# A second sequence's attention placed later in the first feed-forward layer: preparation of its first pair of heads in six steps of its own, its jobs from a third of the layer on

## The chip, the cores and the metric

The kernel runs on one core of a Trainium2 chip. The metric is the device time of one execution in microseconds (us): lower is better. Before the change the median of 3 runs is 1101.23 us.

## What is computed

Attention over 4 sequences of 576 tokens with 8 heads of 64 columns, where a score counts only if it lies within `tau` of its row's greatest, and then two feed-forward layers over the 2304 tokens (512 columns, 2048 hidden):

```python
scores = scale * np.matmul(q, k.transpose(0, 1, 3, 2))
scores = np.where(scores >= max(scores) - tau, scores, -1e9)
attn = softmax(scores)
x = np.matmul(attn, v)                        # to (2304, 512)
h = x @ w_in;  x = (h * clip(h + 3, 0, 6) / 6) @ w_out       # layer 1
h = x @ w2_in; r = maximum(h, 0); out = (r * r) @ w2_out     # layer 2
```

The four weight matrices arrive as 64-bit floats and are turned on the chip into pairs of 16-bit floats, a high and a low part.

## The kernel before, in words

**Attention.** A unit is a pair of heads of one sequence; there are 16, u0 to u3 for the first sequence, u4 to u7 for the second, and so on. A unit has nine jobs (128 queries each, one of them the two heads' tails). `run` (L422) writes the jobs out in steps: step i writes `scores` (L272) and `soft1` (L290) of job i, `soft2` (L305) of job i-1, and `av` (L328) of job i-LAG with LAG = 5. In a job TensorE makes the scores `s` in a PSUM tile of the pool `ps_s`, VectorE takes the row's extreme `nm` (L293), ScalarE the exponential (L303), VectorE the threshold and row sum (L310, which frees `s`), ScalarE and GpSimd the high and low part (L316 to L318), SyncE's queue a transposing DMA into `pt` (L320), and TensorE the product with v (L342).

A unit has to be prepared first (`prep_steps`, L182): TensorE transposes `kraw` and `qraw` (L176) in four parts into tiles called `tps`, ScalarE and VectorE copy them out. In the first sequence units are plain, a copy by ScalarE (L192, L199, L201). From the second sequence on they are kept as a rounded value and a remainder, so each part costs a ScalarE and a VectorE instruction for each head (L212, L213, L222, L223); two DMAs double k (L226), and `prep_v` (L231) scales v. One preparing step is taken for each job of the unit ahead, so u4 is prepared during u3's jobs, and it is handed over from the first `run` to the second (L419, L420). The `tps` tiles of u4, and of u4 alone, come from `ps_s` (L171), three tiles that it shares with `s`; all others come from `ps_a`. A unit's k, q and v are loaded by SyncE's queue (L153 to L168) during jobs 2, 4 and 6 of the unit two ahead: u4's during u2's, u5's during u3's.

**The feed-forward layers.** A block is one layer for one sequence, in the order 1_0, 2_0, 1_1, 2_1 and so on (L752). A block has 16 hidden tiles `hp` (L657) in four quads, and after each quad four output tiles `y` (L694); each tile is 24 matmuls and comes from `ps_s` too. The first hidden tile of the next quad stands ahead of a quad's outputs. Each tile gives two yields, and layer 1 ends with BUBBLE = 8 more yields while its result is scaled and split (L709, L378, L379). That is 72 yields for block 1_0.

**The weights.** In the first sequence's blocks, `tick` (L612) and `want_w` convert a weight tile some tiles ahead of its use: a 1 MB load (L502, L505), VectorE's reduction (L521), a scale by way of TensorE (L118), ScalarE, VectorE, ScalarE and GpSimd instructions (L583 to L595), and a store of 512 KB for the later sequences (L597). Blocks 1_0 and 2_0 convert 16 tiles each; the first two are written out among the last jobs of the first sequence (L769), and after step 34 (L772) four loads and the scaling of the first three quarters of x follow.

**The order of the work.** At L778 41 steps have been written: the 36 jobs of the first sequence and LAG steps more. Then the blocks are written tile by tile, and after each yield `attn_to` (L799) writes as many further steps as an even spread asks for. For block 1_0 the spread is FIRST_ATT = 15 steps over its 72 yields (L789), so that the second sequence's first job is written with the first tile. Block 2_0 gets 26 steps over 56 yields. The framework places each engine's instructions with a schedule of its own, so the order on an engine is near to the written one and not always equal to it.

Of the kernel before, what the change touches and what calls it, by code (L numbers as in the profile page):

```python
# [26 lines left out]
FIRST_ATT = 15  # L27
EARLY = {2: 0, 3: 1, 4: 2, 5: 3, 6: 5, 7: 7}
# [10 lines left out]
def attention_moe_moe_kernel(  # L39
# [130 lines left out]
    def transpose_part(t, part, wide=False):  # L170
        if wide:  # L171
            a = ps_s.tile([P, 2, 512], F32, tag="s", name="tps")[:, 0]
        else:
            a = ps_a.tile([P, 512], F32, tag="acc", name="tps")
        for i, j in enumerate((0, 1) if part == 0 else (2, 3, 4)):
            nc.tensor.transpose(a[:, i * P:i * P + P], t[:, j].rearrange("p h d -> p (h d)"), ident)  # L176
        return a
# [4 lines left out]
    def prep_steps(u):  # L182

        u.plain = u.b == 0
        if u.plain:
# [3 lines left out]
            for part in (0, 1):  # L189
                a = transpose_part(u.k, part, u.i == NPAIR)  # L190
                c0, n = cols(part)
                nc.scalar.activation(out=u.kf[:, c0:c0 + n], in_=a[:, 0:n], func=AF.Copy)  # L192
                yield
            for part in (0, 1):
                a = transpose_part(u.q, part, u.i == NPAIR)
# [11 lines left out]
        for part in (0, 1):  # L207
            a = transpose_part(u.k, part, u.i == NPAIR)
            c0, n = cols(part)
            for h in range(2):  # L210
                kh = u.ks[h][own[h], 0, c0:c0 + n]
                nc.scalar.activation(out=kh, in_=a[own[h], 0:n], func=AF.Copy)  # L212
                nc.vector.tensor_tensor(out=u.ks[h][own[h], 1, c0:c0 + n], in0=a[own[h], 0:n], in1=kh.bitcast(F32), op=ALU.subtract)  # L213
            yield
        for part in (0, 1):
            a = transpose_part(u.q, part, u.i == NPAIR)
# [174 lines left out]
    def attention():  # L391
# [27 lines left out]
        pr = yield from run(us, all_jobs[0:n], None)  # L419
        yield from run(us, all_jobs[n:], pr)  # L420

    def run(us, all_jobs, pr):  # L422
        n = len(all_jobs)
        for i in range(n + LAG):
            if i < n:
                j = all_jobs[i]
                if j.first:
# [3 lines left out]
                    pr = prep_steps(us[j.u.i + 1]) if j.u.i + 1 < len(us) else None  # L431
# [21 lines left out]
            if i < n and all_jobs[i].u.i + 2 < len(us):  # L453
# [8 lines left out]
        return pr  # L462
# [294 lines left out]
    need = {f"1_{b}": (b + 1) * 9 * NPAIR + (LAG if b else 0) for b in range(B)}  # L757
# [21 lines left out]
    for i, (tag, layer, b) in enumerate(blocks):  # L779
# [8 lines left out]
        if i == 0:  # L788
            ng, todo = 4 * NF + BUBBLE, FIRST_ATT  # L789
# [7 lines left out]
        for g, _ in enumerate(moe(tag, layer, b, xs)):  # L797
            if nxt is not None:
                attn_to(min(nxt + LAG, start + math.ceil(todo * (g + 1) / ng)))  # L799
# [30 lines left out]
```

## Time and profile before

| | us |
|---|---|
| median of 3 runs | 1101.23 (1100.09 to 1102.97) |
| the profiled execution | 1104.33 |
| its span (first to last instruction) | 1102.5 |
| first sequence's attention, to the first tile `hp` | 0 to 102 |
| block 1_0 | 102 to 273 |
| block 2_0 | 273 to 422 |

Busy times in the profile are sums over one execution of one engine: PE is TensorE's matmuls, PEld its weight loads, DVE VectorE, ACT ScalarE, POOL GpSimd, and SPq SyncE's queue, which issues nearly all DMAs. PEclk is TensorE's granted clock as a share of its full 2.4 GHz (0.50 is 1.2 GHz). The DMA share is that of the 16 DMA engines, and can pass 1 where transfers overlap. An engine's idle time counts only where something later waits for it.

### The profile page before, as it was taken

How to read it: one execution, taken by the hardware profiler on the slowest of the kernel's cores; microseconds unless marked ns; L12 is line 12 of the kernel's file. 1: busy time of each engine (PE TensorE's matmuls, PEld its weight loads, DVE VectorE, ACT ScalarE, POOL GpSimd, SP SyncE). 2: the span in 40 equal slices, each digit the busy share in tenths (PEclk: the TensorE clock that was granted, in tenths of full speed). 3: DMA queues.
4: the chain of work that ended last, by engine and by line, in shares of the span. 5: the costliest groups of instructions: out<-in, count | busy, mean ns of one | idle time of the engine just before them, and what ended most of it. 6: DMA issues, size and time to landing. Idle time of an engine off the chain costs nothing.

```text
span 1102.5 us, 23355 instructions
## 1 busy us (share of the span) xinstructions
PE 1008.4 (91%) x9248; PEld 817.0 (74%) x9248; DVE 644.1 (58%) x1344; ACT 654.2 (59%) x1128; POOL 500.7 (45%) x613
## 2 busy tenths in 40 slices
PE   6867587986998999999999999999899999998998
PEld 4646465775777878878788888888688887776776
DVE  5788599677778785455855564555835231224122
ACT  6878599676887875655576465755554344213222
POOL 6867178654555763434354443444444212212111
PEclk9998699997999999999999999999999999999999
DMA  6998999787686886665566656556455342222211
GB/s 143 161 215 188 311 277 325 242 257 177 174 207 184 174 204 178 124 146 135 132 134 138 147 139 153 131 120 142 86 129 118 103 130 82 96 77 77 78 39 44
DMA packets 264126, 168.66 MB, mean 153 GB/s; under 512 B 221264, under 2 KB 233552, under 8 KB 264016
## 3 DMA queue, kind: packets, MB, share of 16 engines
q1 hardware_dynamic: 262688, 166.83, 60.7%
q8 instruction: 73, 1.20, 0.5%
q10 hardware_dynamic: 1328, 0.33, 0.1%
q14 instruction: 37, 0.30, 0.1%
HBM read 99.62 MB, written 21.50 MB: 110 GB/s over the span
## 4 chain that ended last, share of the span: by engine, by line
PE 64%; DVE 14%; ACT 8%; DMA 8%; issue 2%; POOL 2%; SPq 1%; ACTq 0%; POOLq 0%; DVEq 0%
PE y L694 28%; PE hp L657 27%; PE s L287 3%; PE o L342 3%; DMA wd<-in_moe_w_in_dram 3%; DVE wc L592 2%; DMA wd<-in_moe_w_out_dram 2%; DVE nm L293 2%; DVE g L521 2%; ACT wc L583 2%; DMA vraw<-in_v_dram 1%; DVE e L310 1%; DVE ya L700 1%; DMA pt<-p 1%; PE tps L176 1%
## 5 line engine op out<-in xcount | busy, mean ns | idle before, releaser
L657 PE MATMUL hp<-x,wpi 128*128 128x288 f16 x3072 | 400.7, 289 | 18.1 <-DVE e L310 5.0
L657 PEld LDWEIGHTS <-wpi 128*128 128x128 f16 x3072 | 298.1, 99 | 97.3 <-issue 9.5
L694 PEld LDWEIGHTS <-wpo 128*128 128x128 f16 x3072 | 296.7, 98 | 85.7 <-issue 6.3
L694 PE MATMUL y<-gh,wpo 128*128 128x288 f16 x2048 | 335.7, 287 | 9.8 <-DVE ya L700 3.5
L668 POOL TENSOR_TENSOR gl<-g,gh 128x576 f16<-128x576 f32 x128 | 168.9, 1322 | 285.0 <-ACT gh L667 284.4
L694 PE MATMUL y<-gl,wpo 128*128 128x288 f16 x1024 | 208.1, 287 | 0.1
L293 DVE TENSOR_REDUCE nm<-s 128x1 f32<-128x576 f32 x144 | 107.9, 751 | 56.3 <-PE s L287 50.6
L700 DVE SCALAR_TENSOR_TENSOR ya<-y,yq,ya 128x576 f32<-128x576 f32 (+1 forms) x97 | 77.8, 808 | 95.3 <-PE y L694 94.8
L318 POOL TENSOR_TENSOR p<-e,p 128x512 f16<-128x512 f32 x108 | 127.1, 1177 | 0.0
L667 ACT ACTIVATE gh<-g 128x576 f16<-128x576 f32 x128 | 86.5, 679 | 57.2 <-DVE g L662 29.2
L310 DVE SCALAR_TENSOR_TENSOR e<-s,thr,e 128x576 f32<-128x576 f32 x108 | 88.0, 815 | 41.7 <-ACT e L303 40.7
L342 PE MATMUL o<-v,pt 128*128 128x64 f16 (+1 forms) x2016 | 92.4, 202 | 13.2 <-DMA pt<-wpo 4.1
L342 PEld LDWEIGHTS <-pt 128*128 128x128 f16 x2016 | 82.4, 101 | 25.0 <-issue 9.4
L316 ACT ACTIVATE p<-e 128x576 f16<-128x576 f32 x108 | 73.6, 682 | 45.5 <-DVE e L310 36.8
L287 PE MATMUL s<-k_st,q_st 128*128 128x288 f32 x480 | 94.1, 319 | 5.7 <-DVE e L310 1.5
L665 DVE TENSOR_TENSOR g<-g,hp 128x576 f32<-128x576 f32 x64 | 48.0, 751 | 66.2 <-ACT g L664 66.0
L661 ACT ACTIVATE g<-hp,r_h,aq 128x576 f32<-128x576 f32 x64 | 52.9, 828 | 55.0 <-PE hp L657 54.5
L662 DVE SCALAR_TENSOR_TENSOR g<-g,r_w,hp 128x576 f32<-128x576 f32 x64 | 51.8, 810 | 54.9 <-ACT g L661 54.8
L664 ACT ACTIVATE g<-hp,r_w 128x576 f32<-128x576 f32 x64 | 47.1, 735 | 59.5 <-PE hp L657 58.4
L317 POOL TENSOR_TENSOR p<-e,p 128x64 f16<-128x64 f32 x108 | 35.0, 324 | 103.0 <-issue 66.2
L303 ACT ACTIVATE e<-s,nm 128x576 f32<-128x576 f32 x108 | 78.3, 725 | 0.4
L287 PEld LDWEIGHTS s<-k_st,q_st 128*128 128x128 f32 x480 | 69.5, 190 | 10.1 <-issue 3.4
(124 smaller groups left out, 1085.0 us busy)
## 6 DMA issues: line engine op xcount, KB each, us to landing
wpi<-scr SPq DMA_DIRECT2D x48, 512.0 KB, 3.8
wpo<-scr SPq DMA_DIRECT2D x48, 512.0 KB, 3.9
wd<-in_moe_w_in_dram SPq DMA_DIRECT2D x16, 1024.0 KB, 6.6
wd<-in_moe_w_out_dram SPq DMA_DIRECT2D x16, 1024.0 KB, 6.5
scr<-wpi SPq DMA_DIRECT2D x16, 512.0 KB, 5.2
scr<-wpo SPq DMA_DIRECT2D x16, 512.0 KB, 4.9
kraw<-in_k_dram SPq DMA_DIRECT2D x16, 256.0 KB, 4.0
vraw<-in_v_dram SPq DMA_DIRECT2D x16, 256.0 KB, 3.2
```

The lines of the kernel that those rows point to most:

```text
L287: nc.tensor.matmul(s[:, half, 0:HALF], lhsT=u.qs[sl][:, cs], rhs=u.ks[sl][:, kk, c], start=i == 0, stop=i == len(ops) - 1)
L293: nc.vector.tensor_reduce(out=j.nm, in_=j.s, axis=AX.XY, op=ALU.min)
L303: nc.scalar.activation(out=j.e, in_=j.s, func=AF.Exp, bias=j.nm, scale=-1.0)
L310: nc.vector.scalar_tensor_tensor(out=j.e, in0=j.s, scalar=j.thr, in1=j.e, op0=ALU.is_le, op1=ALU.mult, accum_out=u.sm[:, col:col + 1])
L316: nc.scalar.activation(out=p16[:, 0:S], in_=e, func=AF.Copy)
L318: nc.gpsimd.tensor_tensor(out=p16[:, S + TAIL:], in0=e[:, 0:NT * P], in1=p16[:, 0:NT * P], op=ALU.subtract)
L342: nc.tensor.matmul(o[:, n * w:n * w + w], lhsT=j.pt[:, c, :], rhs=vv[:, hs, vc, :], start=i == 0, stop=i == len(ops) - 1)
L657: nc.tensor.matmul(hp[:, a, 0:HALF], lhsT=wsl(tag, "i", f, w, c), rhs=x[c][:, a * HALF:(a + 1) * HALF], start=i == 0, stop=i == 3 * NC - 1)
L667: nc.scalar.activation(out=gh, in_=gf, func=AF.Copy)
L668: nc.gpsimd.tensor_tensor(out=gl, in0=gf, in1=gh, op=ALU.subtract)
L694: nc.tensor.matmul(a[:, k_, 0:HALF], lhsT=wsl(tag, "o", f, w, e), rhs=g[f][:, k_ * HALF:(k_ + 1) * HALF], start=i == 0, stop=i == len(ops) ...
L700: nc.vector.scalar_tensor_tensor(out=y, in0=av_, scalar=yq, in1=y, op0=ALU.mult, op1=ALU.add)
```

## The change

The first `run` ends with the first sequence: it neither loads u4 and u5 nor prepares u4. After it come six steps (PRE = 6) that hold no job: the first issues u4's loads of k and q, the next five take the five preparing steps of u4, and four of these also issue, one each, u4's v and u5's k, q and v. Then the second `run` follows as before. In block 1_0 nothing is written of these steps until yield 24 (FIRST_AT, after hidden tile 8, a third of the block); the 6 + 15 steps are spread over the remaining 48 yields. So the first job is written at yield 37. At the end of block 1_0 the same jobs have been written as before, and from block 2_0 on the spread is the same (26 steps over 56 yields). The transposed tiles of u4 come from `ps_a` like all others.

```diff
+FIRST_AT = 24
+PRE = 6
...
-    def transpose_part(t, part, wide=False):
-        if wide:
-            a = ps_s.tile([P, 2, 512], F32, tag="s", name="tps")[:, 0]
-        else:
-            a = ps_a.tile([P, 512], F32, tag="acc", name="tps")
+    def transpose_part(t, part):
+        a = ps_a.tile([P, 512], F32, tag="acc", name="tps")
...
-        pr = yield from run(us, all_jobs[0:n], None)
-        yield from run(us, all_jobs[n:], pr)
-
-    def run(us, all_jobs, pr):
+        yield from run(us, all_jobs[0:n], NPAIR)
+        load_qk(us[NPAIR], "k")
+        load_qk(us[NPAIR], "q")
+        yield (0, 0)
+        nxt = [lambda: load_v(us[NPAIR])] + [lambda x=x: load_qk(us[NPAIR + 1], x) for x in "kq"] + [lambda: load_v(us[NPAIR + 1])]
+        pr = prep_steps(us[NPAIR])
+        for _ in range(PRE - 1):
+            next(pr, None)
+            if nxt:
+                nxt.pop(0)()
+            yield (0, 0)
+        assert next(pr, 1) == 1 and not nxt
+        yield from run(us, all_jobs[n:], len(us))
+
+    def run(us, all_jobs, stop):
         n = len(all_jobs)
+        pr = None
...
-                    pr = prep_steps(us[j.u.i + 1]) if j.u.i + 1 < len(us) else None
+                    pr = prep_steps(us[j.u.i + 1]) if j.u.i + 1 < stop else None
...
-            if i < n and all_jobs[i].u.i + 2 < len(us):
+            if i < n and all_jobs[i].u.i + 2 < stop:
...
-    need = {f"1_{b}": (b + 1) * 9 * NPAIR + (LAG if b else 0) for b in range(B)}
+    need = {f"1_{b}": (b + 1) * 9 * NPAIR + (LAG + PRE if b else 0) for b in range(B)}
...
         if i == 0:
-            ng, todo = 4 * NF + BUBBLE, FIRST_ATT
+            ng, todo = 4 * NF + BUBBLE - FIRST_AT, PRE + FIRST_ATT
...
             if nxt is not None:
-                attn_to(min(nxt + LAG, start + math.ceil(todo * (g + 1) / ng)))
+                x = g + 1 if i else g + 1 - FIRST_AT
+                attn_to(min(nxt + LAG, start + math.ceil(todo * x / ng)))
```

## Rows read from the trace of the kernel before

**Rows 1.** The page's head and busy times of the whole span.

```profile
span 1102.5 us, 23355 instructions
PE 1008.4 (91%) x9248; PEld 817.0 (74%) x9248; DVE 644.1 (58%) x1344; ACT 654.2 (59%) x1128; POOL 500.7 (45%) x613
```

**Rows 2.** Busy time by stretch: PE, PEld, DVE, ACT, POOL; then PEclk, DMA share, GB/s.

```profile
30.00:63.00 33.00, 25.78 (x259) 19.05 (x256) 24.87 (x58) 27.02 (x60) 25.23 (x51) 1.00 0.96 161
63.00:102.00 39.00, 26.93 (x255) 19.45 (x254) 34.03 (x82) 33.36 (x70) 28.20 (x46) 0.87 0.95 208
102.00:129.00 27.00, 16.32 (x163) 13.22 (x162) 17.54 (x38) 14.44 (x26) 10.83 (x17) 0.77 1.03 281
129.00:176.00 47.00, 38.80 (x275) 29.21 (x274) 40.56 (x86) 42.11 (x60) 29.62 (x24) 0.92 0.99 300
176.00:259.00 83.00, 75.06 (x661) 59.83 (x662) 66.69 (x126) 63.16 (x92) 54.18 (x48) 0.96 0.82 246
259.00:273.00 14.00, 5.65 (x55) 4.90 (x53) 11.01 (x31) 9.74 (x13) 6.94 (x7) 0.65 0.82 233
273.00:422.00 149.00, 137.09 (x1369) 113.56 (x1368) 116.45 (x259) 116.96 (x204) 88.92 (x99) 0.99 0.76 182
```

**Rows 3.** Tiles `k_st`, then `q_st`, 63 to 102 us: PE, PEld, DVE, ACT, POOL.

```profile
63.00:102.00 39.00, 0.00 (x0) 0.00 (x0) 1.80 (x4) 1.61 (x4) 0.00 (x0) 0.87 0.95 208
63.00:102.00 39.00, 0.00 (x0) 0.00 (x0) 2.50 (x6) 2.48 (x6) 0.00 (x0) 0.87 0.95 208
```

**Rows 4.** Chain that ended last, 72 to 103 us: start, length, what.

```profile
72.28 0.32 DVE k_st L213
...
91.01 0.47 ACT q_st L222
...
97.92 0.69 SPq L157
...
98.66 2.08 SPq L160
...
100.78 1.99 DMA qraw<-in_q_dram
```

**Rows 5.** Timeline of POOL and SyncE's queue, 97 to 124 us: start, length, what.

```profile
97.59 1.16 POOL L318 TENSOR_TENSOR wpo<-g,wpo 128x512 f16<-128x512 f32 x1
...
101.55 1.32 SPq L320 DMA_TRANSPOSE pt<-wpo  x1
...
106.09 1.28 SPq L168 DMA_DIRECT2D vraw<-in_v_dram  x2
107.41 1.14 SPq L502 DMA_DIRECT2D wd<-in_moe_w_in_dram  x2
...
109.86 13.56 SPq L320 DMA_TRANSPOSE pt<-wpo  x3
```

**Rows 6.** TensorE at the start of block 1_0: two timeline rows, one stretch.

```profile
117.42 0.77 PE L118 MATMUL vm<-ident_m,gm 128*128 128x128 f32 x2 [6.04 <-DVE gm L523]
...
131.58 3.52 PE L657 MATMUL hp<-x,wpi 128*128 128x288 f16 x14 [1.57 <-ACT x L370]
...
118.00:121.00 3.00, 2.86 (x41) 2.75 (x40) 2.44 (x11) 2.56 (x4) 0.00 (x0) 0.50 1.10 317
```

**Rows 7.** Tiles `tps`, `s` (PE, PEld, DVE, ACT), `e`, `vraw` (DVE, ACT, POOL), 129 to 176 us.

```profile
129.00:176.00 47.00, 2.31 (x10) 1.58 (x10) 4.00 (x9) 3.80 (x9) 0.92 0.99 300
129.00:176.00 47.00, 3.62 (x20) 2.78 (x20) 6.20 (x11) 2.96 (x4) 0.92 0.99 300
129.00:176.00 47.00, 3.22 (x7) 5.02 (x7) 4.29 (x6) 0.92 0.99 300
129.00:176.00 47.00, 1.69 (x2) 0.83 (x1) 0.00 (x0) 0.92 0.99 300
```

**Rows 8.** Timeline: SyncE's queue at 139 us, VectorE at 240 us.

```profile
139.32 0.62 SPq L157 DMA_DIRECT2D kraw<-in_k_dram  x1
...
239.66 0.75 DVE L293 TENSOR_REDUCE nm<-s 128x1 f32<-128x576 f32 x1
```

More of the change, by code (lines that the diff above doesn't have):

```diff
@@ L189, in prep_steps @@
             for part in (0, 1):
-                a = transpose_part(u.k, part, u.i == NPAIR)
+                a = transpose_part(u.k, part)
                 c0, n = cols(part)
@@ L194, in prep_steps @@
             for part in (0, 1):
-                a = transpose_part(u.q, part, u.i == NPAIR)
+                a = transpose_part(u.q, part)
                 c0, n = cols(part)
@@ L207, in prep_steps @@
         for part in (0, 1):
-            a = transpose_part(u.k, part, u.i == NPAIR)
+            a = transpose_part(u.k, part)
             c0, n = cols(part)
@@ L215, in prep_steps @@
         for part in (0, 1):
-            a = transpose_part(u.q, part, u.i == NPAIR)
+            a = transpose_part(u.q, part)
             c0, n = cols(part)
@@ L461, in run @@
             yield (i, n)
-        return pr
     wseq = []
```

## Prediction

> **What bounds the kernel now.** I read the page's busy times first. The reader is to see that TensorE is busy for 1008 of 1102 us and no other engine for more than 60% [rows 1]: over the whole span TensorE is the bound, and a change that moves work without removing any can gain only what TensorE stands idle. So the next view is busy time by stretch [rows 2]. From 273 us on TensorE is at 92% and more. Its idle time lies ahead of that: 12 us between 63 and 102, 11 between 102 and 129, 8 each in 129 to 176 and 176 to 259, and 8 at the layer's end (each the length less the PE column). Those are the stretches the change touches; from block 2_0 on the same jobs come at the same spacing, so I carry a difference at 273 us unchanged to the end.
>
> What limits them differs. From 63 to 102 us it is VectorE (34.0 of 39) and ScalarE (33.4) in turn; TensorE does 26.9. The chain of waits runs there through VectorE and ScalarE, then through SyncE's queue [rows 4]. At the start of block 1_0 TensorE waits 6.0 us and a later 1.6 [rows 6]: it has done three quarters of the first tiles and needs the last quarter of x, whose last three transposing DMAs are issued from 109.86 on and take the queue 13.6 us, behind weight loads issued at 107.41 [rows 5]. From 129 to 176 us, from the restart to hidden tile 8, ScalarE is at 42.1 of 47 (90%), with the DMA share at 0.99. From 176 to 259 us TensorE is at 90%, VectorE at 80%, ScalarE at 76%.
>
> **Part A, the preparation of u4 leaves the first sequence (-8 us).** Removed between 63 and 102 us: ten evictions on each engine, ScalarE 1.61 + 2.48 = 4.1 us, VectorE 1.80 + 2.50 = 4.3 us [rows 3], beside them the scaling of v, 1.69 and 0.83 us by the like rows of u5 [rows 7], ten transposes of TensorE, 2.3 us by u5's, and on SyncE's queue 18 load issues and two doubling DMAs. On the chain nine pieces of these evictions lie between 72.28 and 91.01 us; they add up to 4.0 us [rows 4]. Then the queue itself is on it: loading u5's q takes 0.69 + 2.08, and its landing 1.99, 4.8 us together. What that did is seen in the timeline: the low part of a job was ready at 97.59 + 1.16 = 98.75 us and its transposing DMA left at 101.55, 2.8 us late; the weight loads of 107.41 stood behind 1.28 us of u5's v [rows 5]. So the weight loads, and with them the last transposes and the restart at 131.58, come 4.0 + 2.8 + 1.3 = 8 us earlier. Ends: 4 us, if only ScalarE's own 4.1 counts, and 11 (4.0 + 4.8 + 1.3 + 0.8 for the scaling of v). Nothing takes the removed work's place here, so a loss is excluded. That u4's transposes no longer hold one of the three `s` tiles is in the same pieces and is not counted again. Taking them from `ps_a` costs nothing where its other users (products with v, scales) leave a tile free; if they do not, a transpose waits for one eviction, about 0.4 us.
>
> **Part B, no jobs in the first third (-9 us).** In 129 to 176 us the attention had four jobs' first halves and u5's preparation: ScalarE 3.80 + 5.02 + 0.83 = 9.7 us, VectorE 4.00 + 6.20 + 1.69 = 11.9, TensorE 2.31 + 3.62 = 5.9 [rows 7]. Without them ScalarE keeps 42.1 - 9.7 = 32.4, VectorE 28.7, TensorE 32.9 us [rows 2]. If TensorE ran through it would take 33 us (-14). If the DMA engines set the pace it would stay at 47 (0): their share is full, and only three transposes leave them, since the loads come again for u4 and u5. I take TensorE at 87%, between its 83% here and the 90% of the next stretch: 38 us, -9. What now hides the weights' conversion is the quad's matmuls alone.
>
> **Part C, the same work in the last two thirds (+11 us).** Into 176 to 273 us go those amounts and u4's preparation (4.9 us of ScalarE, 6.0 of VectorE, 2.3 of TensorE). Sums: TensorE 75.1 + 5.7 + 5.9 + 2.3 = 89, ScalarE 63.2 + 9.7 + 9.7 + 4.9 = 87.5, VectorE 66.7 + 11.0 + 11.9 + 6.0 = 95.6, in what were 97 us [rows 2, 3, 7]. VectorE becomes the largest. At 87%, its best over a long stretch (34.0 of 39), it needs 110 us, +13. The lower end is TensorE's: 89 at block 2_0's 92% is 97 us, +0. The upper end is VectorE at block 2_0's 78% (116.5 of 149): 122.6 us, +26. I take +11, near VectorE's best, because part B leaves VectorE some 9 us idle (38 less 28.7), into which a little of the weights' conversion can shift.
>
> **What costs nothing.** The six steps add no instruction. The loads of u4 are written one step ahead of their first transposes, and TensorE would wait for them if they were issued there. But the queue runs ahead of the written order: the eighth load of k is issued at 139.32 us, though it is written with the job whose reduction (the 48th) runs at 239.66 [rows 8]. So I expect u4's loads well ahead of their use; if not, some 4 to 5 us of landing stand open once, and this is in the range.
>
> **The sum.** -8 - 9 + 11 = -6 us on the profiled execution's 1104.3, which is 1098.3; that execution is 3.1 us above the median, so the median should go from 1101.2 to 1095. About 0.3%, 3.3 us, is what a measurement of this kernel can tell from no change.
>
> **The rivals.** *The last two thirds absorb it all:* TensorE keeps 92% there, C is 0, and the time is 1101.2 - 17 = 1084. For it: TensorE has 16 us idle after 176 us. Against: three engines would all stand near 90% at once, which no stretch shows. Chance 0.17.
>
> *The gain is not to be had:* the DMA engines hold the first third (B is -4), or u4's loads and transposes slip forward between the first sequence's last jobs, since an engine's order is not the written one (A shrinks by as much). Then the change does in part not what it says, and -8 - 4 + 11, or -4 - 9 + 11, gives 1099 to 1100. For it: the DMA share of 0.99 and the load of rows 8. Against: the share falls to 0.82 after 176 us with as many weights to come. Chance 0.25.
>
> *VectorE becomes the bound of the last two thirds:* there a job comes every 2.3 yields in place of 4.8, VectorE's reductions and threshold passes stand between weight conversion and output sums, and the three `ps_s` tiles are held by `s` twice as often while TensorE waits for VectorE to free them. At block 2_0's 78% C is +26 and the time 1101.2 + 9 = 1110. It decides from C = +20 on, VectorE below 82% (95.6 of 117). For it: block 2_0 has just this density. Against: 80 to 87% in the three stretches before. Chance 0.15.
>
> *The clock falls in the thinner first third.* After TensorE's 6 us wait the clock stood at 0.50, 1.2 GHz [rows 6], and the means of the two stretches around it say what that lost: 0.23 x 27 + 0.08 x 47 = 10 us of full speed [rows 2]. One more such wait, with TensorE at work for most of it, would cost some 9 us, take B back to 0, and give 1104. Against it: from 30 to 63 us TensorE was busy for only 78% and kept 1.00 [rows 2]. Chance 0.06. By the Trainium skill, "TensorE: Matmul & The Clock Gate", section "HAM oscillation — how this bites in real kernels", short bursts of matmuls that wait for loads put the engine at half rate again and again; this rule speaks against thinning out a weight-bound third. The trace agrees that a wait of this size halves the clock, and no run here shows it repeating.
>
> **How the numbers follow.** My forecast has 0.37. Faster by over 0.3%: nearly all of it, the first rival and a little of the second, 0.53. Within 0.3%: the most of the second and the edges, 0.26. Slower: the third, half of the fourth and the unlucky ends (A at 4 with C at 13 or more), 0.21. The range runs from the first rival's 1084 to just short of the third's 1110, 1109.
>
> **What would show it.** Right: the restart near 123 us; 38 us in place of 47 from there to hidden tile 8, TensorE at 87% in it; no `nm` of the second sequence before that tile; block 1_0 ending near 267. Wrong: a restart still past 127 (A), 129 to 176 no shorter with the DMA share still full (B), VectorE below 82% after the first third and waits of TensorE on L310 there (C), or a difference at 273 us that is gone by 422.

## The result: 1110.14 us, slower by 0.7%, and the profile after

The changed kernel takes **1110.14 us** (median of 8 runs, 1105.56 to 1117.86) against 1102.88 for the kernel before on the same chip. The ratio is **1.0073, 95% interval 1.0049 to 1.0097**. The prediction was 1095.0, faster; the range, 1084 to 1109, misses the median by 1 us.

The profiled execution is one of the faster ones, 1106.09 us with a span of 1103.7. A second profile of the same kernel (e4_after_again) took 1110.79 us, so where the two differ the second is nearer to the median.

The busy times of the whole span, against [rows 1]: TensorE does the same work, and no engine's share shows that anything was moved.

```profile
span 1103.7 us, 23366 instructions
PE 1005.2 (91%) x9248; PEld 816.1 (74%) x9248; DVE 643.5 (58%) x1344; ACT 656.8 (60%) x1128; POOL 497.9 (45%) x613
```

By stretch, with the bounds of [rows 2] (PE, PEld, DVE, ACT, POOL, then PEclk, DMA share, GB/s):

```profile
102.00:129.00 27.00, 17.84 (x178) 13.53 (x176) 17.48 (x29) 17.70 (x27) 11.16 (x12) 0.74 1.10 304
129.00:176.00 47.00, 40.08 (x318) 31.04 (x316) 32.82 (x68) 40.76 (x48) 30.80 (x22) 1.00 0.85 290
176.00:259.00 83.00, 68.07 (x573) 54.05 (x571) 67.73 (x142) 62.18 (x96) 46.00 (x46) 0.96 0.80 211
259.00:273.00 14.00, 5.21 (x46) 4.59 (x46) 10.57 (x27) 6.42 (x11) 5.66 (x9) 0.87 1.07 305
273.00:422.00 149.00, 136.50 (x1385) 113.92 (x1386) 119.80 (x275) 122.73 (x217) 93.72 (x103) 0.98 0.78 187
```

TensorE gains in 129 to 176 us (318 matmuls in place of 275, at a clock of 1.00), and gives it back in 176 to 259 (573 in place of 661, 82% busy in place of 90%). The gain of the first third has become idle time of the last two thirds. These bounds are the old kernel's: in the changed kernel the first third runs from 121 to 157 us, and its own stretches are shown under e4.

What follows compares kernels by four marks, three on TensorE and one on VectorE: the *restart* (the first `hp` after the first sequence's last `xT`, 131.58 in [rows 6]), the start of hidden tile 8, the end of block 1_0 (start of the scaling that closes it, VectorE's L709 before), and the first `hp` of block 1_1. Each line below is one profiled execution of one kernel; the ratio at its end is of all its timed runs against the kernel before. A profiled execution can lie some us off its kernel's median (after 4.1 and e10 4.5 below it, e3 3.7, e6 3.4 and e7 5.7 above), so the marks alone settle no difference of a few us.

| kernel | restart | to tile 8 | to the end of 1_0 | block 2_0 | first `hp` of 1_1 | ratio |
|---|---|---|---|---|---|---|
| before | 131.6 | 44.5 | 96.6 | 150.0 | 422.7 | 1 |
| after | 121.1 | 35.9 | 116.3 | 151.8 | 425.1 | 1.0073 |
| e4 after again | 121.1 | 37.9 | 115.5 | 154.6 | 429.1 | |
| e1 no delay | 121.3 | 39.6 | 108.3 | 151.4 | 420.6 | 0.9974 |
| e12 the same again | 120.6 | 39.9 | 106.5 | 150.3 | 417.3 | 0.9961 |
| e2 delay alone | 131.6 | 38.3 | 102.0 | 156.1 | 428.0 | 1.0073 |
| e3 third `p16` | 122.4 | 37.2 | 115.4 | 155.5 | 430.5 | 1.0058 |
| e5 delay 12 | 121.6 | 36.9 | 107.6 | 154.8 | 420.9 | 0.9990 |
| e18 delay 18 | 121.7 | 38.2 | 106.8 | 155.8 | 422.5 | 1.0031 |
| e6 8 steps, not 15 | 120.5 | 36.3 | 96.4 | 174.1 | 427.3 | 1.0078 |
| e7 after, conversion of 12 to 21 out | 121.3 | 35.7 | 100.6 | 155.6 | 413.2 | 0.9899 |
| e8 before, the same out | 130.2 | 44.3 | 84.2 | 153.9 | 412.6 | 0.9926 |
| e9 after, u4 from `ps_s` | 121.8 | 37.5 | 108.7 | 155.5 | 423.5 | 1.0000 |
| e10 after, conversion of 4 to 11 out | 120.5 | 32.3 | 107.5 | 153.4 | 413.7 | 0.9955 |
| e11 no delay, the same out | 121.3 | 42.1 | 95.5 | 152.1 | 411.0 | 0.9901 |
| e13 no delay, u4 from `ps_s` | 122.8 | 41.7 | 102.8 | 152.3 | 419.6 | 1.0008 |
| e14 delay 12, u4 from `ps_s` | 121.2 | 46.0 | 103.5 | 156.8 | 427.5 | 1.0074 |
| e15 before, u4 from `ps_a` | 129.5 | 48.4 | 92.4 | 158.5 | 428.8 | 1.0071 |
| e16 no delay, u4 and u5 from `ps_s` | 123.7 | 44.9 | 99.1 | 156.9 | 424.6 | 1.0045 |
| e17 before, 16 steps | 131.2 | 50.9 | 92.9 | 146.1 | 421.1 | 0.9990 |

Read the first two rows: -10.5 at the restart, -8.6 to tile 8, **+19.7 to the end of block 1_0**, +1.8 in block 2_0 (+4.6 in e4). From the first `hp` of block 1_1 to the last instruction the kernel before takes 679.8 us and the changed one 678.6 (679.6 in e4), so what the change loses is lost before it; over all kernels of the table that rest is 676 to 684 us. The first two terms are much as forecast. The other two are not.

The restart first. On SyncE's queue (start, length, what), against [rows 5]:

```profile
77.76 1.22 SPq L512 DMA_DIRECT2D wd<-in_moe_w_in_dram  x2
79.02 0.67 SPq L159 DMA_DIRECT2D kraw<-in_k_dram  x1
79.74 3.69 SPq L162 DMA_DIRECT2D kraw<-in_k_dram  x2
...
99.57 1.06 SPq L515 DMA_DIRECT2D wd<-in_moe_w_out_dram  x2
...
101.19 0.63 SPq L159 DMA_DIRECT2D qraw<-in_q_dram  x1
...
108.56 7.13 SPq L319 DMA_TRANSPOSE pt<-wpo  x3
```

The weight loads that went out at 107.41 now go out at 77.76, the two behind them at 99.57, and the last three transposing DMAs, no longer right behind four weight loads, take the queue for 7.1 us in place of 13.6. They leave only 1.3 us earlier than before. The loads of u4's k go out at 79.02, 80 us before their first use, and those of its q at 101.19, still ahead of these transposes: a written order of six late steps did not make them late.

### The profile page after: what moved, and what is told of

Its sections match the earlier page's. It is cut to its first block, busy times and chain, and to the rows that moved or that the text cites. A ratio compares the mean times of both kernels' runs of the same rounds, so it can differ in the third digit from the quotient of the medians.

```text
span 1103.7 us, 23366 instructions
## 1 busy us (share of the span) xinstructions
PE 1005.2 (91%) x9248; PEld 816.1 (74%) x9248; DVE 643.5 (58%) x1344; ACT 656.8 (60%) x1128; POOL 497.9 (45%) x613
## 4 chain that ended last, share of the span: by engine, by line
PE 63%; DMA 12%; DVE 12%; ACT 6%; POOL 3%; issue 2%; SPq 1%; POOLq 0%; DVEq 0%; ACTq 0%
PE y L704 27%; PE hp L667 26%; DMA wd<-in_moe_w_out_dram 4%; PE s L286 3%; PE o L341 3%; DMA wd<-in_moe_w_in_dram 3%; DMA pt<-p 2%; DVE nm L292 2%; DVE wc L602 2%; DMA kraw<-in_k_dram 1%; DVE g L531 1%; DVE e L309 1%; DMA pt<-wpo 1%; DVE x L378 1%; DMA vraw<-in_v_dram 1%
## 5 line engine op out<-in xcount | busy, mean ns | idle before, releaser
L678 POOL TENSOR_TENSOR gl<-g,gh 128x576 f16<-128x576 f32 x128 | 166.3, 1300 | 290.0 <-ACT gh L677 289.3
L710 DVE SCALAR_TENSOR_TENSOR ya<-y,yq,ya 128x576 f32<-128x576 f32 (+1 forms) x97 | 77.6, 808 | 93.3 <-PE y L704 92.9
L309 DVE SCALAR_TENSOR_TENSOR e<-s,thr,e 128x576 f32<-128x576 f32 x108 | 87.8, 814 | 40.2 <-ACT e L302 39.4
L341 PE MATMUL o<-v,pt 128*128 128x64 f16 (+1 forms) x2016 | 89.1, 200 | 18.6 <-DMA pt<-wpo 10.0
L341 PEld LDWEIGHTS <-pt 128*128 128x128 f16 x2016 | 79.6, 100 | 30.4 <-DMA pt<-wpo 11.6
```

Source lines behind the costliest of these rows:

```text
L309: nc.vector.scalar_tensor_tensor(out=j.e, in0=j.s, scalar=j.thr, in1=j.e, op0=ALU.is_le, op1=ALU.mult, accum_out=u.sm[:, col:col + 1])
L341: nc.tensor.matmul(o[:, n * w:n * w + w], lhsT=j.pt[:, c, :], rhs=vv[:, hs, vc, :], start=i == 0, stop=i == len(ops) - 1)
L678: nc.gpsimd.tensor_tensor(out=gl, in0=gf, in1=gh, op=ALU.subtract)
L710: nc.vector.scalar_tensor_tensor(out=y, in0=av_, scalar=yq, in1=y, op0=ALU.mult, op1=ALU.add)
```

## The experiments

**The two halves of the change.** The preparation in steps of its own without the delay (e1), the delay without the steps (e2).

```diff
-FIRST_AT = 24
+FIRST_AT = 0
```

> The changed kernel with FIRST_AT = 0: u4 is prepared in its six steps of its own and u4, u5 are loaded late, but the 6 + 15 steps are spread over all 72 yields of block 1_0. Theory (the loss is in the last two thirds, where the jobs that were held back pile up on VectorE and free the weight buffers late): the gain of the first sequence stays, the first tile hp 3 to 4 us earlier than in the kernel before, and there is no pile, so 1096 to 1100 us, 3 to 7 below the kernel before. Rival (moving the preparation of u4 into block 1_0 is itself what costs): as slow as the changed kernel, 1105 to 1112.

Measured: 1099.6 us against 1103.0 on the same chip, ratio **0.9974** (0.9952 to 0.9997). e2 puts the delay alone into the kernel before:

```diff
-            ng, todo = 4 * NF + BUBBLE, FIRST_ATT
+            ng, todo = 4 * NF + BUBBLE - FIRST_AT, FIRST_ATT
...
+                x = g + 1 if i else g + 1 - FIRST_AT
```

> The kernel before, u4 prepared in the first sequence, but its 15 steps in block 1_0 written only from yield 24 on, over 48 yields. Theory (the pile in the last two thirds costs): slower than before, 1104 to 1110 us, since 15 jobs in 48 yields are nearly as dense as the changed kernel's 21 steps, and the gain of the first sequence is missing. Rival (the moved preparation is what costs): the gain of the free first third is kept, 1095 to 1099 us.

Measured: 1111.97 us, ratio **1.0073** (1.0043 to 1.0102), 2 us above the theory's range. The two halves have opposite signs. The restart comes 10 us earlier with the steps and not at all with the delay: that gain belongs to the steps alone. The time to tile 8 is the surprise: 39.6 us with the steps and no delay, in place of 44.5. VectorE's first reduction of the second sequence comes at 157.8 us there, close to tile 8 at 160.9, since six of the 21 steps of block 1_0 hold no job and stand ahead of the others. The steps clear the first third of jobs by themselves; what the delay adds is 2 to 4 us.

e12 ran the winner again, in five rounds.

> The six steps without the delay once more, in five rounds. Theory (taking u4's preparation out of the first sequence gains, the delay is what loses): 1097 to 1101, ratio 0.996 to 0.999, below 1 with its whole interval. Rival (the first gain was chance): 0.999 to 1.001.

Measured: 1098.66 us, ratio **0.9961** (0.9938 to 0.9984). The gain of the steps without the delay holds up, and this is the fastest version that computes everything.

**How much delay.** 12 yields (e5) and 18 (e18) in place of 24.

```diff
-FIRST_AT = 24
+FIRST_AT = 12
```

> The changed kernel with FIRST_AT = 12: nothing of the second sequence is written for a sixth of block 1_0 in place of a third, 21 steps over 60 yields. Theory (what the engines stand idle while no jobs are there is not made up later, so the cost grows with the length of the gap): between FIRST_AT = 0 (1099.6 us) and 24 (1110), so 1102 to 1106. Rival (the density of the last two thirds passes a limit, VectorE's, only at 21 steps in 48 yields): as FIRST_AT = 0, 1098 to 1101.

> The changed kernel with a delay of 18 yields, between 12 (0.999) and 24 (1.0073). Theory one (the delay has a price that grows with it): 1.002 to 1.006. Theory two (the time answers to where single jobs fall among the weights' work): anything from 0.997 to 1.009, as likely outside the two as between them; a value under 0.999 or over 1.0075 speaks for it.

Measured: 1101.42 us, ratio 0.9990 (0.9973 to 1.0007), and 1105.49 us, 1.0031 (1.0015 to 1.0047); e5 falls between its two forecasts. With no delay, 12, 18 and 24 yields the ratios are 0.997 (0.996), 0.999, 1.003 and 1.007: with everything else as in the changed kernel the delay has a price, and it grows with the delay, as theory one of e18 had it. Where it is paid changes. Up to 18 yields the stretch to the end of block 1_0 stays at 106.5 to 108.3 us and block 2_0 takes 155 or 156 in place of 150 or 151; at 24 the stretch jumps to 116. The three stretches of e18 and of e12 (restart to tile 8, to the end of 1_0, block 2_0), first e18:

```profile
121.70:159.90 38.20, 34.42 (x245) 25.89 (x245) 25.53 (x55) 31.41 (x37) 20.32 (x15) 0.87 0.93 304
159.90:266.70 106.80, 84.75 (x746) 68.32 (x744) 92.80 (x199) 87.05 (x134) 60.22 (x63) 0.96 0.92 253
266.70:422.50 155.80, 140.48 (x1389) 115.85 (x1387) 119.49 (x266) 120.34 (x212) 90.42 (x100) 0.96 0.76 178
```

and the same stretches of e12, without the delay:

```profile
120.60:160.50 39.90, 36.16 (x262) 27.90 (x262) 31.86 (x73) 35.56 (x48) 18.79 (x14) 0.90 0.97 297
160.50:267.00 106.50, 85.78 (x740) 68.16 (x737) 91.32 (x187) 84.79 (x126) 67.81 (x66) 0.91 0.92 254
267.00:417.30 150.30, 139.80 (x1376) 115.45 (x1377) 116.28 (x262) 118.33 (x207) 91.77 (x100) 0.97 0.79 182
```

The delay buys 1.7 us to tile 8 here and costs 5.5 in block 2_0, into which it pushes 13 matmuls and 5 ScalarE instructions. In the changed kernel these are 35 and 12 (the x columns of its block 2_0, shown under e4).

**Is it the density of the held-back steps?** e6 keeps the delay and writes 8 of the 15 steps in block 1_0.

```diff
-FIRST_ATT = 15
+FIRST_ATT = 8
```

> The changed kernel with FIRST_ATT = 8 in place of 15: still nothing for a third of block 1_0, then 14 steps over 48 yields, the density of FIRST_AT = 0 (0.29 steps a yield); seven jobs more go into block 2_0. Theory (work held back has to be made up where there is no room, and block 2_0 has none): block 1_0 ends 6 to 12 us earlier than in the changed kernel, block 2_0 is as much longer, 1107 to 1112 us in all. Rival (only the density of the last two thirds of block 1_0 is at fault): 1096 to 1102 us.

Measured: 1109.98 us, ratio 1.0078 (1.0052 to 1.0105). The total is the theory's, the shift is larger than its 6 to 12 us. Block 1_0 now ends at 253.2, 20 us earlier than in the changed kernel, and block 2_0 takes 174.1 us in place of 151.8: 22 us more. Seven steps are worth 20 / 7 = 2.9 us each where they are taken out and 22 / 7 = 3.2 where they are put in. Block 2_0 has no free room for them, although TensorE is idle for 12 us of it.

**Is it one buffer?** At the end of block 1_0 the chain of the changed kernel (start, length, what) runs through a weight load, a transposing DMA behind it and ScalarE's `p16`.

```profile
258.93 8.34 DMA wd<-in_moe_w_out_dram
...
267.34 6.03 DMA pt<-p
...
273.40 0.68 ACT p L315
```

e3 gives `p16` a third buffer.

```diff
-            p16 = at.tile([P, 2 * S], F16, name="p16")
+            p16 = at.tile([P, 2 * S], F16, name="p16", bufs=3)
```

> The changed kernel with three p16 tiles in place of two. At the end of block 1_0 the chain of the changed kernel runs through a weight load, a transposing DMA behind it, and ScalarE's wait for a p16 tile ahead of the scaling of x. Rival theory (that wait at the layer's end is the loss): block 2_0 starts 4 to 6 us earlier and the time falls to 1103 to 1106 us. Theory (the pile on VectorE and the late weight loads): no more than 2 us better, 1108 to 1111.

Measured: 1109.29 us, ratio 1.0058 (1.0035 to 1.0081); block 1_0 ends at 275.0. The buffer gives back nothing that can be told from chance. The unchanged kernel was run beside it:

> The changed kernel as it is, for a second trace: its runs spread from 1105.6 to 1117.9 us while the kernel before stays within 1100.1 to 1104.2. Theory: the first two thirds are the same to 1 us in both traces and the spread arises between hidden tile 8 and the start of block 2_0, in the time of the weight loads. Rival: it arises after block 2_0's start, by a lower granted clock through the rest.

Measured: 1110.79 us. Its three stretches, and after them those of the first profile, of the changed kernel:

```profile
121.00:159.00 38.00, 34.18 (x240) 25.44 (x240) 25.33 (x53) 31.09 (x37) 19.33 (x15) 0.86 0.91 296
159.00:274.50 115.50, 87.08 (x726) 69.06 (x725) 92.90 (x195) 85.43 (x126) 63.59 (x62) 0.96 0.83 232
274.50:429.10 154.60, 141.04 (x1412) 117.13 (x1413) 121.34 (x271) 123.54 (x219) 92.09 (x103) 0.97 0.77 183
```

```profile
121.00:157.00 36.00, 32.28 (x240) 24.39 (x240) 25.18 (x52) 30.75 (x37) 19.11 (x15) 0.93 0.92 308
157.00:273.30 116.30, 86.94 (x726) 69.00 (x724) 93.23 (x198) 85.50 (x126) 63.76 (x62) 0.95 0.84 233
273.30:425.10 151.80, 139.59 (x1411) 116.59 (x1412) 119.72 (x271) 123.45 (x219) 93.55 (x103) 0.98 0.77 185
```

The same three of the kernel before:

```profile
131.60:176.10 44.50, 37.94 (x272) 28.77 (x271) 39.20 (x86) 40.64 (x58) 28.12 (x23) 0.94 0.98 298
176.10:272.70 96.60, 80.41 (x712) 64.43 (x713) 77.34 (x152) 72.61 (x103) 60.99 (x54) 0.92 0.82 245
272.70:422.70 150.00, 138.09 (x1375) 114.52 (x1376) 116.72 (x261) 117.76 (x207) 89.05 (x99) 0.99 0.76 182
```

The middle stretch of the changed kernel is the same in both profiles to 1 us, with the same matmuls: the 116 us are the kernel's, not an execution's. Neither forecast of e4 holds: the first third differs by 2.0 us and block 2_0 by 2.8, with the same matmuls but one. In the first third e4 has TensorE wait 3.76 us for VectorE, and the clock, which had come back to 1.00 between 125 and 127 us, falls again behind that wait:

```profile
128.84 7.43 PE L667 MATMUL hp<-x,wpi 128*128 128x288 f16 x36 [3.76 <-DVE g L672]
...
130.00:135.00 5.00, 5.00 (x24) 3.13 (x22) 2.97 (x5) 2.74 (x5) 5.00 (x5) 0.53 0.72 203
```

In the first profile that wait is 2.06 us, and the clock is 1.00 from 130 to 157 us.

**Is it the weights' conversion?** e7 and e8 leave out the conversion of weight tiles 12 to 21 (loaded and reduced as before; a finished 16-bit tile is fetched in their place), in the changed kernel and in the one before.

```diff
+        if 12 <= k < 22:
+            w = new_w(kind)
+            nc.sync.dma_start(out=w, in_=w16s[(1, kind, 0)])
```

> The changed kernel without the conversion of ten weight tiles, numbers 12 to 21, which fall into the last two thirds of block 1_0 and the start of 2_0: they are still loaded and reduced, but the tile used is a stored one of the first layer, fetched by one DMA (that part of the result is another one). To be read against the kernel before with the same left out. Theory (the held-back jobs collide with the weights' conversion on ScalarE and VectorE and with the weight buffers that it frees): without these conversions there is room, and this kernel is 3 to 9 us faster than its partner. Rival (the jobs' own chain through TensorE's order and the three s tiles is the limit): still 4 to 9 us slower than its partner.

> The partner of the run above: the kernel before without the conversion of the same ten weight tiles. Theory and rival both expect it well below the kernel before, by 8 to 20 us, since 34 us of ScalarE's and 14 us of VectorE's work fall away while TensorE's stays; they differ in whether the changed kernel with the same left out comes out faster (theory, by 3 to 9 us) or slower (rival, by 4 to 9 us) than this one.

Measured: 1091.67 us, ratio 0.9899 (0.9872 to 0.9926), and 1094.02 us, 0.9926 (0.9901 to 0.9951). Without these conversions the changed kernel is no longer the slower one; it is 2.3 us the faster, less than the theory's 3 to 9, and the intervals overlap. But the stretch to the end of block 1_0 is still 100.6 us against 84.2, 16.4 more, where with the conversions it was 19.7 more. So by these profiles (e7's is the slowest of its four executions) the conversion of the last two thirds is only a small part of what that stretch lost, and its engine is not the bound either: in e7 ScalarE is busy for 54.81 of these 100.6 us, and the held-back jobs are still slow.

```profile
157.00:257.60 100.60, 85.02 (x725) 68.62 (x722) 80.50 (x188) 54.81 (x98) 38.27 (x54) 0.96 0.95 269
```

e10 and e11 leave out the conversion of tiles 4 to 11 in the same way, in the changed kernel and in the one without delay.

> The changed kernel with the conversion of weight tiles 4 to 11 left out (they are still loaded and reduced, and a finished 16-bit tile is fetched in their place). Theory (after the restart TensorE itself sets the pace of the first third: busy for 27.8 of the 29.4 us from restart to hidden tile 8): that stretch stays at 28 to 30 us, the restart stays near 127, and the time falls only by what is freed after tile 8, 2 to 6 us, to 1104 to 1108. Rival (the first third is paced by the weights' loop of load, reduction and conversion): the stretch falls to 25 or 26 us or the restart comes 3 us earlier, and the time falls to 1102 or less.

> The same left out of the kernel with the six steps but no delay. Theory (TensorE sets the pace of the first third, the delay costs later): 1093 to 1097, and the delayed kernel stays some 10 us behind this one, as it does with the conversions in (1110 against 1099.6). Rival (the weights' loop is what left the delay without gain): with the conversions gone the delayed kernel draws ahead in the first third, and the gap between the two falls to 5 us or less.

Measured: 1098.54 us, ratio 0.9955 (0.9938 to 0.9972), and 1093.33 us, 0.9901 (0.9875 to 0.9927). Neither theory holds whole. From hidden tile 3 at 125.9 to tile 8 at 152.8 e10 takes 26.9 us, between the two forecasts, and TensorE is busy for all of them; the total fell by some 12 us, as the rival said. The kernel without delay gained 5 to 8 us, by the medians or the ratios, and the gap between the two went from over 10 to 5 or 6. The held-back kernel pays about twice as much for these conversions; most of it appears after tile 8 (116.3 to 107.5 us, and 106.5 to 95.5 without the delay), not in the third that holds them.

**Is it the pool of u4's transposed tiles?** e9 undoes this part of the change alone.

```diff
-        a = ps_a.tile([P, 512], F32, tag="acc", name="tps")
+        if wide:
+            a = ps_s.tile([P, 2, 512], F32, tag="s", name="tps")[:, 0]
+        else:
+            a = ps_a.tile([P, 512], F32, tag="acc", name="tps")
```

> The changed kernel with one part undone: u4's transposed tiles come from ps_s again, as before. In the changed kernel TensorE waits 2.8, 2.0 and 0.9 us in block 1_0's last two thirds for VectorE to empty k_st pieces out of ps_a. Theory (these waits belong to what the last two thirds lost): they go, block 1_0 ends 2 to 4 us earlier (270 to 272) and the time is 1105 to 1108. Rival one (the waits move to the next late thing, VectorE's other work): the end of 1_0 stays at 273 to 275, 1108 to 1111. Rival two (u4's tiles now take ps_s from the jobs and hidden tiles at a time when there are more of them): 1_0 ends later than 275, 1112 or more.

Measured: 1103.97 us against 1103.79, ratio **1.0000** (0.9978 to 1.0022), below the changed kernel's interval and below the theory's 1105 to 1108. Block 1_0 ends at 268.0. The stretch that had taken 116 us takes 108.7 with four matmuls more:

```profile
159.30:268.00 108.70, 89.13 (x730) 69.56 (x727) 94.02 (x193) 83.70 (x124) 62.36 (x60) 0.94 0.83 246
```

Which waits went? The waits of TensorE from 157 to 275 us (engine, line, what it waited for, us in all, times, longest), of the changed kernel, with one line left out:

```profile
PE tps L175 <- DVE k_st L212: 4.8, 2, 2.8
PE s L286 <- DVE sm L325: 4.6, 1, 4.6
PE hp L667 <- DVE e L309: 3.9, 2, 2.6
PE xT L358 <- DMA pt<-p: 3.5, 1, 3.5
...
PE s L286 <- DVE e L309: 2.3, 2, 1.7
```

and of e9 (its lines stand up to three further down in the kernel):

```profile
PE tps L178 <- DVE mx L122: 3.1, 2, 1.8
PE tps L178 <- ACT xr L375: 2.9, 1, 2.9
PE tps L178 <- DVE ya L713: 2.9, 1, 2.9
PE o L344 <- DMA pt<-p: 2.5, 1, 2.5
```

Of the two waits for `k_st` only the longer is u4's; the other is u5's, whose tiles come from `ps_a` in every kernel but e16. Both are gone in e9, but inside block 1_0 other waits of transposes have come, 3.1 and 2.9 us (the third, 2.9 for `xr`, ends at 271.18, behind the block). What is really absent from e9 are the two long ones at the layer's end, 4.6 and 3.5 us. There the chain of e9 runs through a weight load and transposing DMAs too, but the load stands at 249.31 us (7.12 us long), in place of 258.93. Part of the gain is lost again: of 5.3 us at the end of block 1_0, 2.6 are left at block 2_0's first hidden tile (272.17 against 274.80), and 1.6 at the first `hp` of 1_1 (5.6 against e4). So the pool is shown to matter here by 7 or 8 us, by the stretch and by the ratio, but not by the way that its own waits suggest.

Four more kernels asked whether the pool has a price of its own.

> The kernel before with one part of the change alone: u4's transposed tiles from ps_a. There u4 is prepared in the first sequence, where VectorE and ScalarE are the busiest and no held-back jobs press. Theory (the pool costs only where u4 is prepared beside block 1_0's weights and jobs): no difference, ratio 0.998 to 1.002. Rival (a pool of two tiles is too small anywhere): 1.003 or more, with the first hidden tile 2 to 4 us later than at 102.

> The six steps without the delay, with u4's transposed tiles from ps_s as before. Theory one (the pool costs only where held-back jobs press, because then VectorE empties the pieces late): no change against the six steps alone, 1097 to 1101, ratio 0.996 to 0.998. Theory two (the pool costs wherever u4 is prepared beside the weights' scaling, whose tiles vm share ps_a): 1092 to 1096, ratio 0.990 to 0.994. Rival (u4's tiles in ps_s hold up the hidden tiles and outputs of the first third): 1101 or more.

> The six steps with a delay of 12 yields and u4's transposed tiles from ps_s. With the pool ps_a this delay gave 0.999, no delay 0.997, 24 yields 1.007; with ps_s 24 yields gave 1.000. Theory one (the delay costs only through the pool): 0.996 to 0.998, level with no delay. Theory two (the delay costs a few us by itself, about 0.1 us for each yield): 0.997 to 1.000, and between no delay and 24 yields.

> The six steps without the delay, with the transposed tiles of u4 and u5 from ps_s. If what the pool gives back is u4's place ahead of the first job, this is level with e13_prep_wide or 1 to 3 us slower, as u5's tiles take ps_s from jobs already under way. If ps_a is short in all of block 1_0, it is 2 to 4 us faster than e13_prep_wide.

Measured: e15 1110.5 us, ratio 1.0071 (1.0052 to 1.0090); e13 1102.71, 1.0008 (0.9994 to 1.0021); e14 1110.49, 1.0074 (1.0061 to 1.0087); e16 1106.81, 1.0045 (1.0032 to 1.0058). e13 came out as its rival had it, the other three not as forecast: e14 lies outside both ranges, e16 is 4 us slower than e13 where 1 to 3 was the most expected, and in e15 the ratio is the rival's, but the first hidden tile is 6 us earlier (96.0), not later. Side by side with the earlier ones:

| u4's transposed tiles from | no delay | 12 yields | 24 yields |
|---|---|---|---|
| `ps_a` (as in the change) | 0.997, 0.996 | 0.999 | 1.007 |
| `ps_s` (as before) | 1.001 | 1.007 | 1.000 |

The pool has no price that can be added to a sum, and neither has the delay: with the six steps and `ps_s`, 24 yields stand level with none, so the price that grows with the delay is that of the kernels with `ps_a`; without the six steps (e2) 24 yields cost 0.7% with `ps_s` too. The table of marks says where each side loses. With `ps_s`, and u4 prepared inside the first third, the time to tile 8 goes up: 41.7, 46.0 and 44.9 us in e13, e14 and e16, against 37 to 40 with `ps_a`. There the transposes share the three tiles with `hp` and `y`, which may be the reason; no wait was traced to it. With 24 yields u4 comes after tile 8, that cost is gone (37.5), and what remains is the gain in the stretch behind it. In the kernel before, with u4 still in the first sequence, `ps_a` brings the restart forward by 2.1 us (129.5) and block 1_0's end by 2.4, yet block 2_0 then takes 158.5 us in place of 150.0, and that alone makes e15 slow. About half of these 8.5 us is TensorE's busy time with the same matmuls (142.2 against 138.1 us, granted clock 0.96 against 0.99). Why block 2_0 answers so is not settled.

Last, how much does a harmless shift do? e17 writes one step more in block 1_0 of the kernel before.

> The kernel before with one step more of the second sequence's attention in block 1_0 (16 in place of 15), and so one fewer in block 2_0. Theory one (the parts of the change have prices of their own): this shift of one job in 72 yields costs or gains next to nothing, 0.998 to 1.002. Theory two (any small shift of the jobs moves the end of block 1_0 and block 2_0 by some us, whatever its direction): off 1 by 0.003 to 0.008, on either side, with block 2_0 at 153 us or more if slower.

Measured: 1099.86 us, ratio 0.9990 (0.9979 to 1.0002). The marks inside the block move by several us (tile 8 at 182.1, the end of 1_0 at 275.0, block 2_0 146.1 us long), and the total does not. So not every small shift costs, and a mark in the middle is no verdict: only the first `hp` of block 1_1 goes, roughly, with the ratio through the table.

## Why the prediction was wrong, step by step

**Part A, right, a little small, by another path on the queue.** Forecast -8 with the restart near 123; measured -10.5, 121.1. That it comes from taking u4's preparation away is shown: e2, which leaves u4 where it was, has none of it (131.6). The working is right only in that SyncE's queue is the place. It took 4.0 us off the evictions on the chain, but the low part of the first sequence's last job is ready at 108.87 us, as before at 108.86 (POOL's rows, first before, then after):

```profile
107.70 1.16 POOL L318 TENSOR_TENSOR wpo<-g,wpo 128x512 f16<-128x512 f32 x1
...
107.26 1.61 POOL L317 TENSOR_TENSOR wpo<-g,wpo 128x512 f16<-128x512 f32 x1
```

And the last transposes leave only 1.3 us earlier, still behind u4's q and v. The queue is through with them 7.7 us earlier (115.69 for 123.42): the four weight loads no longer stand right ahead of them, having left 9 and 30 us earlier, not 8. Of the 18 load issues that the prediction counts between 63 and 102 us, 15 lie there; u5's v comes behind.

**Part B, right in size, wrong in its owner.** Forecast 47 to 38 us, -9; measured 44.5 to 35.9 in the first profile and 37.9 in e4, so -8.6 and -6.6. TensorE is busy for 90% of it, the DMA share stays at 0.92 and 0.91 (0.98 before) while the stretch shortens, so the engines of the DMA did not hold it at 47, and no `nm` came before tile 8. But the text put the whole of B down to the delay. e1 and e12 have it for -4.9 and -4.6 without any: the six steps stand in the place of the jobs. The delay's own part is 2 to 4 us, and the sum set the whole of B against C, which is what the delay costs.

**Part C is the step that failed.** Forecast +11, measured +19.7 (18.9 in e4). With it the end of block 1_0, forecast 6 us earlier, comes -10.5 - 8.6 + 19.7 = 0.6 us later, and 1.8 later in e4. Its working gave 97 to 123 us and chose 108, near the 110 of VectorE at 87%; the stretch took 116.3, with VectorE at 80%. Without the delay and with 12 or 18 yields the stretch does take 106.5 to 108.3 us, and with u4's tiles in `ps_s` it takes 108.7 at 24 yields too. The choice near VectorE's best therefore held for these neighbours of the kernel (VectorE at 84 to 87% in e1, e12, e18 and e9), and not for it. Two sentences led astray. One is "taking them from `ps_a` costs nothing ... about 0.4 us": at 175.65 us a transpose of u4 waits 2.83 us for VectorE to empty a piece of `k_st`. (At 203.31 another waits 1.96; that one is u5's, which this edit does not touch.)

```profile
161.44 0.38 PE L175 MATMUL tps<-ident,kraw 128*128 128x128 f32 x2
...
175.65 0.41 PE L175 MATMUL tps<-ident,qraw 128*128 128x128 f32 x2 [2.83 <-DVE k_st L212]
...
203.31 0.44 PE L175 MATMUL tps<-ident,qraw 128*128 128x128 f32 x2 [1.96 <-DVE k_st L212]
```

The tile it needs was filled at 161.44, and its four evictions end 14 us later, because ScalarE (L601, L593) and VectorE (L531, L602) convert and reduce weights between them. ScalarE's two copies of it start at 166.45 and 171.69 (the second row has the next tile's first copy with it), and VectorE's last one is the first of the two at 175.08:

```profile
166.45 0.36 ACT L211 ACTIVATE k_st<-tps 64x256 fp32r<-64x256 f32 x1
...
171.69 0.83 ACT L211 ACTIVATE k_st<-tps 64x256 fp32r<-64x256 f32 x2
...
175.08 0.94 DVE L212 TENSOR_TENSOR k_st<-tps,k_st 64x256 fp32r<-64x256 f32 x2
```

An eviction was costed by its own length; what counts is how long its engine takes to come to it. Undoing this edit is worth some 7 us of C, more than this wait; how the rest comes about is not shown. The other sentence let VectorE's idle time of the first third take up some of the conversion. VectorE was indeed idle there (25.2 of 36 us busy), and the stretch behind it was no shorter for that.

**"From block 2_0 on ... unchanged", wrong.** This term was put at nothing and measured 1.8 us, 4.6 in e4. A difference of 0.6 us at the end of block 1_0 (1.8 in e4) is 2.4 (6.4) at the start of block 1_1. The same number of jobs had their reductions before that end as in the kernel before (15), but not their later halves: block 2_0 got 36 matmuls, most of them one job's product with v, and 12 ScalarE instructions more than in e1. The deferred work crosses the block's edge although the count of written steps does not. In e2 block 2_0 is nearly the whole loss (-6.2 to tile 8, +5.4 after it, +6.1 in block 2_0), but with one matmul more: there it is mostly the clock, as the last section shows.

**The loads ahead of their use, right.** u4's k loads left at 79.02 us, so no landing stood open.

**The rivals.** The third one gives 1110, which is what was measured, and two of its signs are there: VectorE at 93.2 of 116.3 us, 80%, and C close to its +20. Its mechanism is there in part only: the waits of TensorE on the threshold pass L309 are 3.9 + 2.3 = 6.2 us of 29.4 idle. That its total was met is in part luck: its sum has +26 for C and nothing for block 2_0, against 19 to 20 and 2 to 5 measured, and e9 shows that some 7 us of C go with the pool, which it does not name. The first rival (the last two thirds absorb it all) was far off: e6 shows about 3 us for each step, in either block. The second fell with the restart at 121 and the shorter first third, although u4's loads did slip forward into the first sequence (from 79.02 us on); its transposes did not. The fourth came true once, at a small price: the clock was 1.00 from 130 to 157 us in the first profile, but in e4 it fell again behind a wait of 3.76 us (0.53 from 130 to 135), and the stretch was 2 us longer, not 9.

**What stays open.** That the delay loses in this kernel with u4's tiles from `ps_a` is settled, by e1, e12, e5, e18 and the change itself; that the pool decides 7 us of it, by e9. By what path the two together lose them, why the same pool costs 0.7% in the kernel before, and why it pays with no delay, was not found. The two long waits at the layer's end that e9 lacks were not tried by themselves.

## What to carry to other kernels

Before work is held back to clear a stretch, ask what else already clears it: six empty steps did half of it or more here, and the delay was left with a gain of 2 to 4 us there and, by the ratios, a net loss of some 3, 7 and 12 us at 12, 18 and 24 yields. Steps moved to the next block saved about 3 us each in one and cost as much in the other (e6). Two edits that share a pool or an engine's order do not add, so run each alone and both together before keeping either; here half of the change was the best complete kernel of the study and the whole was slower than doing nothing. An eviction that frees a buffer is priced by how long its engine takes to reach it, not by its own length.

## What the runs showed of the hardware

What had not been expected is that a short wait in block 2_0 can cost twice. TensorE waits there around 300 us for VectorE to free a tile. In the kernel before that wait is 1.9 us and the clock stays up; in e2 it is 3.6 us and the clock goes to the lower of its two levels for a few us behind it. The row of the wait and the 5 us windows around it, first of the kernel before:

```profile
299.12 0.67 PE L694 MATMUL y<-gh,wpo 128*128 128x288 f16 x4 [1.89 <-DVE e L310]
...
300.00:305.00 5.00, 4.85 (x61) 4.01 (x59) 3.81 (x7) 4.10 (x7) 3.55 (x5) 1.00 1.18 283
305.00:310.00 5.00, 5.00 (x43) 4.17 (x42) 2.50 (x7) 4.07 (x11) 2.84 (x4) 1.00 0.68 141
```

then of e2:

```profile
302.00 1.14 PE L695 MATMUL y<-gh,wpo 128*128 128x288 f16 x4 [3.64 <-DVE e L311]
...
300.00:305.00 5.00, 3.00 (x13) 1.94 (x14) 4.46 (x10) 4.68 (x9) 2.41 (x4) 0.61 0.85 269
305.00:310.00 5.00, 5.00 (x51) 3.74 (x50) 1.40 (x4) 1.66 (x4) 2.19 (x5) 0.70 0.79 173
```

The means of 0.61 and 0.70 say that the clock was at 1.2 GHz for much of these 10 us and at 2.4 for the rest. Over block 2_0, TensorE is busy for 142.3 us in e2 (granted clock 0.95) and 138.1 in the kernel before (0.99) with one matmul between them: 4.2 us of its 6.1 are clock, 1.9 are idle time. The length of the wait alone does not decide it: waits of 2.43 and 2.49 us in the first profile of the changed kernel (ending at 301.98 and 360.11) left the clock at 1.00, and one of 2.21 in e2 (at 361.62) brought it down. The two profiles of the changed kernel differ there in the same way with one matmul between them (141.0 and 139.6 us busy), which fits the wide spread of its runs. By the Trainium skill, "TensorE: Matmul & The Clock Gate", section "HAM oscillation — how this bites in real kernels", bursts of matmuls that wait for loads are run at half rate again and again. The trace agrees in part: in the first third, which the change thins out, the clock fell a second time in e4 (0.53) and not in the first profile (1.00), and the waits ahead of these dips, there and in block 2_0, are on VectorE and not on loads; over block 2_0 TensorE is busy for more than 90%.
